# k times v as one product a head in two column groups: an RWKV-5 block with a feed-forward, on one core

## The chip, the cores and the metric

The kernel runs on one core of one Trainium2 chip. The metric is device time in microseconds (us) of one execution. The program has 24 units of work (four batches by six chunks of 128 tokens). Engines are named as the profile names them: PE is TensorE's matmuls, PEld its weight loads, DVE is VectorE, ACT ScalarE, POOL GpSimd, SP SyncE.

## The reference

```python
# attention: r, k, v of shape (4, 8, 768, 48); w, u of shape (8, 48)
state = np.zeros((B, H, D, D))
for t in range(S):
    cur = np.einsum('bhd,bhe->bhde', u[None] * kt, vt)
    y[:, :, t] = np.einsum('bhd,bhde->bhe', rt, state + cur)
    state = w[None, :, :, None] * state + np.einsum('bhd,bhe->bhde', kt, vt)
# then, on x of shape (3072, 384): h = x @ w_in (384 x 1024), SoLU, layer norm, ln @ w_out (1024 x 384)
```

The kernel works chunk by chunk. Within a chunk of 128 tokens the attention is a masked score matrix times v. Between chunks it carries a state of 48 by 48 a head, to which each chunk adds k (decayed) times v.

## The kernel before

Heads are padded from 48 to 64 columns in k and r, so that two heads fill the 128 partitions. The state of a pair of heads is a tile of 128 partitions by 2 x 48 columns, with each head's block on the diagonal. The rest of it must be zero, because y multiplies the whole tile. The product of k and v was taken for a pair of heads at once. Half of its result is one head's k with the other's v, and the weight tile `wt`, zero off the diagonal, removes it.

```python
def make_wt():                                   # called once, in the second step
    nc.gpsimd.memset(wt, 0.0)
    for q in range(2):
        rows = slice(q * P, q * P + D)
        nc.gpsimd.tensor_copy(out=wt[rows, :, q, :],
                              in_=pw[rows, 0, 7].unsqueeze(2).to_broadcast([D, HP, D]))
# ... in finish(i), after y_ps:
if c < C - 1:
    kv_ps = psM.tile([128, HP, 2, D], F32, tag="m", name="kv_ps")
    for a in range(HP):                          # four pairs of heads
        nc.tensor.matmul(kv_ps[:, a], pair(X["kp"], a), vt[:, 2 * a : 2 * a + 2, 0:D],
                         start=True, stop=True)
    if c > 0:
        nc.vector.tensor_add(St, kv_ps, St)
        nc.gpsimd.tensor_mul(St, St, wt)
    else:
        nc.vector.tensor_mul(St, kv_ps, wt)
# ... the order of one step of the loop, on TensorE:
# tr_ps, tk_ps (transposes of r and k), t_ps (of solu), h_ps, at (scores), o_ps, y_ps, kv_ps
```

## Time and profile before

| | before |
|---|---|
| median of 5 runs | 427.5 us (427.41 to 427.6) |
| span in the profile, mean granted clock | 425.5 us, 0.984 |
| TensorE busy | 396.0 us, 93% |
| kv_ps on the chain that ended last | 1.06 us a unit, 13 times |

The page has each engine's busy time, and the chain of work that ended last, followed back from the end. Two rows of such views carry the argument: a row of the busy table (a stretch of time, then busy us of each engine) says which engine is full, and a row of the chain (start, us, what) says what a piece of work costs where it counts. The prediction below shows these lines.

### The profile page before, as it was taken

To read this page: it belongs to the slowest core of one execution; us is meant where nothing else is said; L and a number is where in the kernel's file an instruction comes from. 1 tells how busy PE (TensorE), PEld (TensorE's weight loads), DVE (VectorE), ACT (ScalarE), POOL (GpSimd) and SP (SyncE) were. 2 spreads that over 40 slices of the span, in tenths; PEclk is the share of its full clock that TensorE was granted. 3 is DMA by queue.
4 is the path that set the end of the run, shared out by engine and by line. 5 is a ranking of instruction groups with operands and counts; after the bars stand their busy time and mean duration, and the time that the engine had idled before them with its cause. 6 is when DMAs were issued, how large, how long until landed. Compare 5 with 4: busy or idle time off the path is not lost.

```text
span 425.5 us, 7222 instructions
## 1 busy us (share of the span) xinstructions
PE 396.0 (93%) x2873; PEld 250.3 (59%) x2873; DVE 157.5 (37%) x302; ACT 181.6 (43%) x424; POOL 146.7 (34%) x220
## 2 busy tenths in 40 slices
PE   2699698879999999999999999999999999999994
PEld 2576255545756656656656656666666655556662
DVE  5988566635332352242242242242242321122110
ACT  1965666662524524525525525525525522233210
POOL 4886556556244144144135135135131100111000
PEclk9999899997999999999999999999999999999998
DMA  8999794000123034034034034034000000000101
GB/s 167 284 182 254 136 166 76 20 2 0 28 47 76 24 52 76 20 56 76 19 56 76 14 62 76 6 70 75 2 18 20 19 2 20 19 20 18 37 18 46
DMA packets 81592, 25.92 MB, mean 61 GB/s; under 512 B 76557, under 2 KB 79758, under 8 KB 81550
## 3 DMA queue, kind: packets, MB, share of 16 engines
q1 hardware_dynamic: 81406, 25.18, 29.6%
q8 instruction: 24, 0.39, 0.4%
q10 hardware_dynamic: 144, 0.20, 0.2%
q14 instruction: 18, 0.15, 0.1%
HBM read 20.65 MB, written 4.72 MB: 60 GB/s over the span
## 4 chain that ended last, share of the span: by engine, by line
PE 78%; DVE 9%; ACT 8%; POOL 2%; issue 2%; DMA 1%; ACTq 0%; POOLq 0%
PE o_ps L816 30%; PE h_ps L774 24%; PE y_ps L744 7%; PE t_ps L805 5%; PE at L716 4%; ACT AT L691 3%; PE kv_ps L760 3%; DVE ma L524 2%; PE tk_ps L705 2%; DVE ma L526 2%; PE tr_ps L697 2%; DVE AT L719 1%; DVE mag L520 1%; DVE solu L786 1%; ACT e L788 1%
## 5 line engine op out<-in xcount | busy, mean ns | idle before, releaser
L774 PE MATMUL h_ps<-w_in_sb,xT 128*128 128x512 f32 x288 | 129.6, 599 | 4.0 <-DVE solu L786 4.0
L816 PE MATMUL o_ps<-w_out_sb,lnT 128*128 128x384 f32 x384 | 129.5, 491 | 0.0
L816 PEld LDWEIGHTS o_ps<-w_out_sb,lnT 128*128 128x128 f32 x384 | 71.2, 190 | 47.5 <-issue 1.0
L774 PEld LDWEIGHTS h_ps<-w_in_sb,xT 128*128 128x128 f32 x288 | 53.4, 193 | 63.1 <-issue 62.2
L719 DVE COPY_PREDICATED AT<-later,at 128x512 f32<-128x512 uint32 x48 | 32.1, 721 | 92.0 <-ACT e L777 89.0
L777 ACT ACTIVATE e<-h_ps 128x1024 f32<-128x1024 f32 x24 | 24.6, 1023 | 89.9 <-PE h_ps L774 89.9
L691 ACT ACTIVATE AT<-ident,own 128x128 f32<-128x128 f32 x192 | 58.4, 386 | 0.8 <-DVE own L685 0.8
L788 ACT ACTIVATE e<-solu 128x1024 f32<-128x1024 f32 x24 | 25.4, 1057 | 71.0 <-DVE solu L786 71.0
L790 POOL TENSOR_TENSOR st<-st 128x1 f32<-128x1 f32 x24 | 4.7, 194 | 139.6 <-DVE solu L786 139.6
L716 PEld LDWEIGHTS at<-rT,kT 48*128 48x128 f32 x384 | 25.7, 198 | 18.7 <-issue 15.5
L763 DVE TENSOR_TENSOR state<-kv_ps,state 128x384 f32<-128x384 f32 x16 | 8.9, 557 | 69.8 <-PE kv_ps L760 69.8
L674 POOL TENSOR_TENSOR kp<-kpad,kdec 128x512 f32<-128x512 f32 x24 | 31.7, 1323 | 5.1 <-ACT kdec L591 4.9
L764 POOL TENSOR_TENSOR state<-state,wt 128x384 f32<-128x384 f32 x16 | 16.1, 1006 | 47.5 <-DVE state L763 47.5
L716 PE MATMUL at<-rT,kT 48*128 48x128 f32 x384 | 30.7, 298 | 1.6 <-DVE AT L719 1.4
L786 DVE SCALAR_TENSOR_TENSOR solu<-h_ps,st,e 128x1024 f32<-128x1024 f32 x24 | 30.8, 1284 | 1.1
L807 DVE COPY lnT<-t_ps 128x512 f32<-128x512 f32 x24 | 16.4, 683 | 36.5 <-PE t_ps L805 36.5
L744 PE MATMUL y_ps<-AT,vt 128*32 128x128 f32 x768 | 27.6, 279 | 0.0
L819 ACT ACTIVATE o<-o_ps,st 128x384 f32<-128x384 f32 x24 | 13.6, 569 | 29.1 <-PE o_ps L816 14.0
L805 PE MATMUL t_ps<-ident,solu 128*128 128x128 f32 x192 | 25.9, 279 | 0.0
L706 ACT COPY kT<-tk_ps 128x512 f32<-128x512 f32 x24 | 14.0, 584 | 25.2 <-PE tk_ps L705 25.2
L805 PEld LDWEIGHTS t_ps<-ident,solu 128*128 128x128 f32 x192 | 22.6, 144 | 2.7 <-issue 2.0
L681 POOL TENSOR_TENSOR rku<-rku,rpad 128x384 f32<-128x384 f32 x23 | 23.3, 1015 | 1.8
(80 smaller groups left out, 378.8 us busy)
## 6 DMA issues: line engine op xcount, KB each, us to landing
kpad<-in_k_dram SPq DMA_DIRECT2D x24, 192.0 KB, 4.2
rpad<-in_r_dram SPq DMA_DIRECT2D x24, 192.0 KB, 4.0
vt<-in_v_dram SPq DMA_DIRECT2D x24, 192.0 KB, 4.1
out_dram<-o SPq DMA_DIRECT2D x24, 192.0 KB, 2.1
raw<-in_moe_w_in_dram SPq DMA_DIRECT2D x6, 512.0 KB, 5.5
raw<-in_moe_w_out_dram SPq DMA_DIRECT2D x8, 384.0 KB, 4.3
u_bc<-in_u_dram ACTq DMA_DIRECT2D x1, 192.0 KB, 3.8
wq<-in_w_dram SPq DMA_DIRECT2D x1, 1.5 KB
```

What stands on the lines that cost most here:

```text
L674: nc.gpsimd.tensor_mul(X["kp"].rearrange("p h d -> p (h d)"), kpads[i % NLD].rearrange("p h d -> p (h d)"), kdec.rearrange("p a d -> p (a ...
L681: engine.tensor_mul(rku, rku, rpads[i % NLD][:, :, 0:D])
L691: nc.scalar.activation(out=AT[:, h, :], in_=ident, func=ACT.Copy, scale=X["own"][:, h])
L716: nc.tensor.matmul(pss[q][:, a, :], X["kT"][rows, a, :], X["rT"][rows, a, :], start=True, stop=True)
L719: nc.vector.copy_predicated(A4[:, :, q, :], later.to_broadcast([128, HP, T]), pss[q])
L744: nc.tensor.matmul(y_ps[32 * g : 32 * g + 32, j, :], lhsT, rhs, start=(g not in opened), stop=stop, skip_group_check=True)
L774: nc.tensor.matmul(h_ps[:, ts(n, NX)], X["xT"][:, j, :], w_in_sb[:, j, ts(n, NX)], start=(j == 0), stop=(j == KD - 1))
L777: nc.scalar.activation(out=e, in_=h_ps, func=ACT.Exp, accum_out=sums[:, i : i + 1])
L786: nc.vector.scalar_tensor_tensor(out=solu, in0=X["h"], scalar=rs, in1=X["e"], op0=ALU.mult, op1=ALU.mult, accum_out=tot)
L788: nc.scalar.activation(out=X["e"], in_=solu, func=ACT.Square, accum_out=ss)
L805: nc.tensor.transpose(t_ps[:, f, :], X["solu"][:, ts(4 * g + f, 128)], ident)
L816: nc.tensor.matmul(o_ps, X["lnT"][:, f, :], w_out_sb[:, f, :], start=(f == 0), stop=(f == KF - 1))
```

## The change

One product a head: 64 columns of k (48 and 16 of padding) by 48 columns of v. The two heads of a pair go to the two halves of the partitions, which are two column groups of the array (a column group is a block of its columns that takes weights and products of its own; how the array is divided is called its tiling mode). Below, "drain" is the time in which earlier products finish before a change of mode, and an "exposed" weight load is one that no product hides. No block across heads is computed, so the weight tile isn't needed, but the states must now be zeroed once, and each half of the state is updated by itself.

```diff
-    wt = const.tile([128, HP, 2, D], F32, name="wt")
-    def make_wt(): ...                                        # cut
+    for St in states:
+        nc.gpsimd.memset(St, 0.0)
@@ finish
-            kv_ps = psM.tile([128, HP, 2, D], F32, tag="m", name="kv_ps")
+            kv_ps = psM.tile([128, HP, D], F32, tag="m", name="kv_ps")
             for a in range(HP):
-                nc.tensor.matmul(kv_ps[:, a], pair(X["kp"], a), vt[:, 2 * a : 2 * a + 2, 0:D],
-                                 start=True, stop=True)
-            if c > 0:
-                nc.vector.tensor_add(St, kv_ps, St)
-                nc.gpsimd.tensor_mul(St, St, wt)
-            else:
-                nc.vector.tensor_mul(St, kv_ps, wt)
+                for q in range(2):
+                    nc.tensor.matmul(kv_ps[ts(q, P), a], X["kp"][:, 2 * a + q, :],
+                                     vt[:, 2 * a + q, 0:D], start=True, stop=True)
+            for q in range(2):
+                wT = pw[ts(q, P), 0, 7].unsqueeze(2).to_broadcast([P, HP, D])
+                S = St[ts(q, P), :, q]
+                if c > 0:
+                    nc.vector.tensor_add(S, kv_ps[ts(q, P)], S)
+                    nc.gpsimd.tensor_mul(S, S, wT)
+                else:
+                    nc.vector.tensor_mul(S, kv_ps[ts(q, P)], wT)
```

More of the change, by code (lines that the diff above doesn't have):

```diff
@@ L602, in direct_path @@
     states = [const.tile([128, HP, 2, D], F32, name=f"state{b}") for b in range(B)]
-    wt = const.tile([128, HP, 2, D], F32, name="wt")
-    def make_wt():
-        nc.gpsimd.memset(wt, 0.0)
-        for q in range(2):
-            rows = slice(q * P, q * P + D)
-            nc.gpsimd.tensor_copy(out=wt[rows, :, q, :],
-                                  in_=pw[rows, 0, 7].unsqueeze(2).to_broadcast([D, HP, D]))
+    for St in states:
+        nc.gpsimd.memset(St, 0.0)
     N = len(units)
@@ L857, in direct_path @@
             weigh(i + 3, nc.gpsimd)
-        if i == -1:
-            make_wt()
         if i == 10:
```

## The prediction

> **What bounds the kernel now.** I read the page first: its first two parts and the chain that ended last. Then I read the busy table by stretch, the chain in order of time, and last the timeline around one product of k and v. On the page (columns: engine, busy us, share of the span, instructions) the matmul engine stands alone, and most of the chain is its work:
>
> ```profile
> PE 396.0 (93%) x2873; PEld 250.3 (59%) x2873; DVE 157.5 (37%) x302; ACT 181.6 (43%) x424; POOL 146.7 (34%) x220
> PE 78%; DVE 9%; ACT 8%; POOL 2%; issue 2%; DMA 1%; ACTq 0%; POOLq 0%
> ```
>
> The busy table by stretch (columns: stretch, its length, busy us of each engine, granted clock, DMA share, GB/s) says where that holds. From 98 us on TensorE is never idle, and VectorE, ScalarE and GpSimd are busy for a third of the time or little more:
>
> ```profile
> 98.00:114.00 16.00, 16.00 (x89) 10.22 (x91) 8.70 (x12) 6.02 (x15) 9.58 (x11) 0.89 0.00 0
> 114.00:323.00 209.00, 209.00 (x1623) 132.70 (x1618) 65.52 (x121) 87.32 (x209) 70.36 (x104) 1.00 0.25 47
> 323.00:425.00 102.00, 96.41 (x546) 57.47 (x536) 18.32 (x36) 28.37 (x55) 6.01 (x20) 0.99 0.06 23
> ```
>
> Before 98 us the chain is a mix of VectorE, ScalarE and GpSimd work, with no piece of the k-times-v product (kv_ps) on it. After that it is TensorE alone, one period per unit of 16.08 us (columns: start, us on the chain, what):
>
> ```profile
> 179.25 1.06 PE kv_ps L760 x8
> 180.31 0.44 PE tr_ps L697 x4
> 180.75 0.44 PE tk_ps L705 x4
> 181.19 0.87 PE t_ps L805 x8
> 182.06 5.15 PE h_ps L774 x12
> 187.21 1.09 PE at L716 x16
> 188.30 5.36 PE o_ps L816 x16
> 193.66 1.67 PE y_ps L744 x56
> ```
>
> There are 20 units with a kv product (five chunks of four batches). The chain in order of time has it 13 times, at 114.95, 131.02 and so on to 307.86 us. So what the change is worth is 13 times what it takes off the 1.06 us, plus whatever it does to the mixed start.
>
> The timeline around one of them (start, us, engine, line, what; the bracket is idle time before it) shows why eight small matmuls take 1.06 us:
>
> ```profile
> 194.16 0.90 PEld L744 LDWEIGHTS y_ps<-AT,vt 128*32 128x32 f32 x32
> 195.25 0.97 PEld L760 LDWEIGHTS kv_ps<-vt,kp 128*128 128x128 f32 x8 [0.20 <-issue]
> 196.12 0.47 PEld L697 LDWEIGHTS tr_ps<-ident,rpad 128*128 128x128 f32 x4
> ```
>
> Each fp32 product appears as two weight loads and two matmuls, so 4 products are 8 pairs. Eight loads take 0.97 us and the last one lasts 0.192 (the median of the rows for kv_ps), so one starts every (0.97 - 0.192) / 7 = 0.111 us. The streamed operand is 96 columns. The 384-column products of o_ps take 5.36 / 16 = 0.335 us on the chain, or 0.87 ns a column, so 96 columns need about 0.084 us. **The weight load of 128 columns sets the pace, not the stream.** In the y_ps row, 32 loads into four column groups take 0.90 us: eight rounds of four, one round every (0.90 - 0.11) / 7 = 0.113 us. Four groups therefore run at once. The score products, with two row groups, do the same: 16 loads in the 0.97 us of 8.
>
> **What the Trainium skill says.** (1) "TensorE: Matmul & The Clock Gate", LDWEIGHTS: the load lasts about P/1.2 ns, where P is the number of columns, whatever the contraction. That is 107 ns for 128 columns; the trace agrees with its pitch of 111. It is 53 ns for 64. The durations agree with the slope: 0.110 us for 32 columns against 0.192 for 128 is 0.85 ns a column. (2) "TensorEngine Tiling (Array Packing)", Key Properties: tiles load and multiply independently, and changing the tiling mode drains the engine. The rounds of four in y_ps agree with the first; the 0.20 us of idle before the kv loads, just after the 32-column mode, with the second. (3) "VectorE: DVE Perf Modes", on the errata: an fp32 two-tensor op takes (N + 151) / 0.96 ns. For N = 384 that is 557 ns, and the trace has 557 for the state sum. (4) "PSUM — Partial Sum Buffer", bank collisions: different column tiles may write one bank at the same time on disjoint partitions. That is what the new kv_ps asks for, and what y_ps does already with 32 columns.
>
> **The change part by part.**
>
> TensorE. It removes 4 products a unit, 128 columns of k by 96 of v, of which half (one head's k by the other's v) was thrown away. It adds 8 products, 64 columns of k by 48 of v, alternating between two column groups: 16 pairs in place of 8.
> - Stream: 48 columns at 0.87 ns are 0.042 us. Load: half of 107 ns plus the 4 ns by which the pitch exceeds it, 0.058 us. The load still sets the pace within a column group.
> - Each group has 8 pairs, 8 x 0.058 = 0.46 us. I take the two groups to run side by side, as the four of y_ps do.
> - Around this: the drain after y_ps, which is there today too. From the end of the last y stream to the first kv load I read about 0.09 us (the last y matmul starts at 195.05 and streams 0.107). Then comes a **new** mode change, from 64-column tiles to the full array of the transposes: about 0.04 for the last stream, 0.09 of drain, and an exposed weight load of the first transpose, about 0.06.
> - Sum from the end of the y stream to the first transpose's stream: 0.09 + 0.46 + 0.04 + 0.09 + 0.06 = 0.74 us. Today the same stretch is 195.16 to 196.22, which is 1.06. **Gain 0.32 us a unit; 13 of them on the path make 4.1 us.**
>
> VectorE. One op of 557 ns on 128 x 384 becomes two on 64 x 192; columns count, partitions do not. By the formula each is (192 + 151) / 0.96 = 357 ns. Consecutive ops overlap by about 0.09 (the 558 ns sum starts at 180.35 and the next op at 180.82), so the pair takes 0.27 + 0.36 = 0.63 against 0.56: 0.07 more, on an engine idle for two thirds of the steady stretch. The sum can start 0.4 earlier, as its matmuls end earlier.
>
> GpSimd. 1.006 us for 384 columns and 1.295 for 512 give 2.26 ns a column and 0.14 fixed. Two of 192 are about 1.14 us: 0.13 more, and nothing on the path waits for them before the next chunk of that batch, four units later. The four zeroings of the states (four of about 0.42, the measured zeroing of the weight tile of the same size) fall before the first decay of k at 8.84 us, where GpSimd waits 4.9 us. The weight tile's three ops at 21.8 to 23.1 us go, but the next op waited for a load that landed at 23.32, so their time turns into waiting. Both worth about nothing.
>
> Start. Up to 98 us VectorE, ScalarE and GpSimd set the pace, so an earlier kv gains nothing. Once, at 82.5 us, the k transpose on TensorE waits. The page names GpSimd, but the transpose also waits on VectorE, whose state sum ends at 82.45, the kv buffer being reused. There the pair of ops costs up to 0.07 on the path. I charge 0.1 us.
>
> Total: 427.5 - 4.1 + 0.1 = **423.5 us**, or 0.9% less.
>
> **The rivals.**
>
> (a) The two 64-column groups do not overlap, or 16 pairs are limited by issue. Then kv takes 16 x 0.058 = 0.93 us plus the new drain, 1.21 in all: 0.15 worse, times 13, about 429.5 us. For it: more instructions, and no 64-column tile in this trace. Against it: y_ps sustains a pair every 0.113 / 4 = 0.028 us, and the new product needs one every 0.029.
>
> (b) A 64-column load costs no more than a 32-column one, since its halves go in at once; then the stream of 42 ns sets the pace: 8 x 0.044 = 0.35, another 0.11 a unit, 422.1 us. Nothing in the trace favours it beyond the four-way overlap in y_ps.
>
> (c) A new wait: the second half of the solu transposes (t_ps) takes the PSUM buffer of kv_ps and so waits for VectorE. Its load waits on VectorE's semaphore at 197.43 today, and the state sum ends at 196.98, a margin of 0.44. After the change TensorE arrives about 0.32 earlier, at 197.11. The last kv matmul should be visible to VectorE at about 195.97, so the pair ends at about 196.6: margin 0.5. This bites only if a half takes over 0.6 us. If it did, most of the gain would be lost and the time would be 426 to 427.
>
> (d) The gain is real and far larger because the path also shortens at the start: against it, no kv piece before 98 us on the chain. A gain of 2% needs 8.6 us, or 0.65 on each of 13 units; the products would have to take 0.4 us including two drains.
>
> **Range and chances.** Rival (b) and a little luck at the start give 421.7; a dearer mode change (0.1 more on 13 units) and some loss at the start give 425.5. I widen slightly to 421.5 to 426.0. Two per cent faster is out of reach of the sum (0.03). Two per cent slower would need rival (a) much worse than worked out (0.02). The rest, 0.95, is within 2%.
>
> **What would show it.** In the profile after: the chain's period of 16.08 us should be about 15.76, with kv_ps at about 0.5 and a larger share for the transpose after it. Weight loads of 64 columns should last about 0.137 us (0.110 + 32 x 0.85 ns), and 16 of them take about 0.55 us on the timeline, in pairs side by side. An idle time before the loads of tr_ps should appear, about as large as the one before kv_ps. The state ops should show 0.36 us on VectorE, and no idle time at t_ps. The start should reach the TensorE-bound stretch at 98 us as now. The prediction is wrong if the 16 loads take about 1 us (a), if t_ps gets a wait on the state (c), or if the stretch before 98 us moves by more than a microsecond.

## The result, and the profile after

The changed kernel took 423.53 us, the median of 5 runs (423.33 to 423.92), against 427.5 beside it. The ratio is 0.9904, with a 95% interval of 0.9891 to 0.9918. A ratio here is the mean time of one kernel's fast runs over that of the other's fast runs of the same rounds, so it is not quite the ratio of the medians. The difference is clear of the noise, and smaller than 2%.

The engines' line and the chain's shares, from the page of the changed kernel:

```profile
PE 388.5 (92%) x3033; PEld 242.2 (57%) x3033; DVE 162.8 (39%) x322; ACT 181.3 (43%) x424; POOL 147.5 (35%) x237
PE 77%; DVE 10%; ACT 5%; issue 3%; POOL 2%; DMA 1%; ACTq 0%; POOLq 0%
```

TensorE has 160 more matmuls (eight a unit) and 7.5 us less busy time; VectorE has 5.3 us more. The busy table shows the same bound as before: TensorE never idles from 98 us to 323 us.

```profile
98.00:114.00 16.00, 16.00 (x82) 10.08 (x84) 8.78 (x12) 5.74 (x14) 9.51 (x11) 0.89 0.00 1
114.00:323.00 209.00, 209.00 (x1783) 131.30 (x1772) 70.12 (x137) 89.83 (x214) 70.85 (x117) 1.00 0.25 48
```

The chain in order of time, one period of it (start, us, what):

```profile
178.30 0.60 PE kv_ps L754 x16
178.90 0.59 PE tr_ps L690 x4
179.49 0.44 PE tk_ps L698 x4
179.92 0.87 PE t_ps L802 x8
...
192.40 1.67 PE y_ps L737 x56
194.06 0.60 PE kv_ps L754 x16
```

The kv piece went from 1.06 to 0.60 us, and the transposes behind it went from 0.44 to 0.59: that 0.15 is the new change of tiling mode. Everything else in the period is as it was. The timeline of the weight loads shows both (start, us, engine, line, what, and idle time before it):

```profile
177.13 0.89 PEld L737 LDWEIGHTS y_ps<-AT,vt 128*32 128x32 f32 x32
178.23 0.55 PEld L754 LDWEIGHTS kv_ps<-vt,kp 128*64 128x64 f32 x16 [0.20 <-issue]
178.83 0.42 PEld L690 LDWEIGHTS tr_ps<-ident,rpad 128*128 128x128 f32 x4
```

Sixteen loads take 0.55 us and each lasts 0.138, so eight rounds of two start every (0.55 - 0.138) / 7 = 0.059 us: the two groups run side by side.

Over 11 periods, from the ninth kv product to the last, the period is 16.076 us before and 15.767 after. That is 0.309 less, and 13 times it is 4.0 us. The times differ by 3.97. But the start is **not** as before. The timeline of the first microseconds has this on GpSimd and VectorE of the changed kernel:

```profile
3.71 1.49 POOL L604 MEMSET state<- 128x384 f32 x4
```

```profile
4.44 0.94 DVE L580 COPY tab<-pw 128x4 f32<-128x4 f32 x1
4.51 0.86 DVE L577 TENSOR_TENSOR pw<-pw 128x4 f32<-128x4 f32 x1
4.59 0.79 DVE L578 RECIPROCAL pw<-pw 128x4 f32<-128x4 f32 x1
```

and on VectorE of the kernel before:

```profile
4.32 0.17 DVE L580 COPY tab<-pw 128x4 f32<-128x4 f32 x1
```

A copy of four columns took 0.94 us in place of 0.17, with the two ops behind it, and it ended just after GpSimd's zeroings did. So the first decay of k started at 9.72 in place of 8.84 us. The product of the column means, which comes just before the TensorE-bound part, started at 97.64 in place of 96.67. Then most of this was given back by the clock. That product runs after 4 us of idle TensorE. In the profile before, the granted clock was 0.50 during it; in the profile after it was 0.88. Below are the chain's line for it and the busy table for just that stretch (the third number from the end is the granted clock), first before, then after:

```profile
96.67 1.65 PE mean_ps L659 x2
96.67:98.32 1.65, 1.65 (x3) 0.94 (x4) 0.00 (x0) 0.00 (x0) 0.00 (x0) 0.50 0.00 0
```

```profile
97.64 0.96 PE mean_ps L652 x2
97.64:98.60 0.96, 0.96 (x3) 0.65 (x4) 0.00 (x0) 0.00 (x0) 0.00 (x0) 0.88 0.00 0
```

The first transposes of the TensorE-bound part follow at 98.32 before and 98.60 after. The start therefore lost 0.97 us, of which 0.28 was left. The last scaling of an output (o) starts at 419.58 before and 415.85 after: 3.73 us, which is 4.0 less 0.28.

### The profile page after: what moved, and what is told of

Same layout as the page of the kernel before. It is cut to its first block, busy times and chain, and to the rows that moved or that the text cites. A ratio compares the mean times of both kernels' runs of the same rounds, so it can differ in the third digit from the quotient of the medians.

```text
span 421.8 us, 7597 instructions
## 1 busy us (share of the span) xinstructions
PE 388.5 (92%) x3033; PEld 242.2 (57%) x3033; DVE 162.8 (39%) x322; ACT 181.3 (43%) x424; POOL 147.5 (35%) x237
## 4 chain that ended last, share of the span: by engine, by line
PE 77%; DVE 10%; ACT 5%; issue 3%; POOL 2%; DMA 1%; ACTq 0%; POOLq 0%
PE o_ps L813 30%; PE h_ps L771 24%; PE y_ps L737 7%; PE t_ps L802 5%; PE at L709 4%; DVE ma L524 2%; ACT AT L684 2%; PE tr_ps L690 2%; PE tk_ps L698 2%; DVE ma L526 2%; PE kv_ps L754 2%; DVE mag L520 2%; DVE AT L712 1%; DVE solu L783 1%; ACT e L785 1%
## 5 line engine op out<-in xcount | busy, mean ns | idle before, releaser
L760 DVE TENSOR_TENSOR state<-kv_ps,state 64x192 f32<-64x192 f32 x32 | 11.4, 355 | 63.6 <-PE kv_ps L754 63.0
L761 POOL TENSOR_TENSOR state<-state,pw 64x192 f32<-64x192 f32 x32 | 16.1, 504 | 39.8 <-DVE state L760 38.6
L673 POOL TENSOR_TENSOR rku<-kpad,u_bc 128x384 f32<-128x384 f32 x23 | 23.5, 1021 | 0.0
```

What stands on the lines that cost most here:

```text
L673: engine.tensor_mul(rku, kpads[i % NLD][:, :, 0:D], u_bc)
```

## The experiments

All eleven runs gave correct results. They ran in three groups, each group on one chip beside the kernel before. Each is the changed kernel with the edit shown; run 5 has none. The theory: the gain is made on TensorE alone, by weight loads half as wide in two groups that run at once, less a new mode change, and the zeroing costs time at the start. The rivals are named with each run.

### 1. The old products, the new halves

```diff
+            kv_ps = psM.tile([128, HP, 2, D], F32, tag="m", name="kv_ps")
             for a in range(HP):
+                nc.tensor.matmul(kv_ps[:, a], pair(X["kp"], a), vt[:, 2 * a : 2 * a + 2, 0:D], start=True, stop=True)
# the halves read kv_ps[ts(q, P), :, q]
```

> The four products of 128 by 96 columns are put back; the halves of the state and the zeroing of the states at the start stay. Theory (the gain is the matmul engine's alone, and the zeroing costs up to 0.9 us at the start because it blocks a VectorE copy): 427.5 to 428.4 us, kv_ps back to 1.06 us a unit on the chain. Rival (the gain comes from the state update by halves or from the removed weight tile): clearly under 427 us.

Measured: 427.56 us, beside 427.27 for the kernel before; ratio 1.0012 (0.9999 to 1.0025). The period is 16.076 us again, kv_ps 1.06 us on the chain. So nothing of the gain comes from the halves, from the lost weight tile or from GpSimd.

### 2. The zeroing moved to where the weight tile was made

```diff
-    for St in states:
-        nc.gpsimd.memset(St, 0.0)
@@ the loop
+        if i == -1:
+            for St in states:
+                nc.gpsimd.memset(St, 0.0)
```

> The changed kernel, with the four zeroings of the states moved from about 3.7 us to where the weight tile was made before (about 22 us). Theory (VectorE's small table copy at 4.4 us took 0.94 instead of 0.17 us because GpSimd's zeroings held a port that both need): the copy is back to about 0.17 us, the k transposes start 0.8 to 0.9 us earlier, and the time falls by 0.3 to 0.9 us to 422.6 to 423.2. Rival (the late start is chance, or is absorbed before 98 us): 423.5 us.

Measured: 424.2 us, ratio 0.9929 (0.9916 to 0.9941). The expectation missed. The copy did take 0.17 us again and k's decay started at 8.89 us, but the gain was lost at 22 us. The timeline there:

```profile
21.82 1.49 POOL L855 MEMSET state<- 128x384 f32 x4
...
21.98 1.60 DVE L520 TENSOR_SCALAR mag<-mag 128x512 f32<-128x512 f32 x1
```

The scaling `mag` takes 0.53 us in the kernel before and 0.40 in the changed one; here it took 1.60 and ended 0.28 us after the last zeroing. The same stall came back at another place. It isn't peculiar to zeroing: in the kernel before, the next `mag`, at 23.61 us, took 1.52 us behind GpSimd's decay of k (23.32 to 24.85 us).

The Trainium skill tells of the mechanism, which I had not looked up when I predicted. In "SBUF — State Buffer", Who interferes with whom, it says that VectorE's copies and scalings can use a port pair that GpSimd shares, and that whoever issues first holds the pair and the other blocks fully. Both stalls fit that: a copy and a scaling, each begun behind a zeroing. The page adds that ScalarE never waits. That is tried in run 8.

### 3. One column group after the other

```diff
-            for a in range(HP):
-                for q in range(2):
+            for q in range(2):
+                for a in range(HP):
```

> The changed kernel, with the eight products in another order: all four of the first column group, then all four of the second. Theory A (each column group takes its instructions as soon as it is free, whatever the order of the program): kv_ps stays at 0.60 us and the time at 423.5. Theory B (matmuls start in program order, so overlap needs alternation): the second group waits for the first, 0.46 us more on 13 units, 429.5 us; half of that if only some of the pairs can pass.

Measured: 426.75 us, ratio 0.9995 (0.9982 to 1.0008). The chain has

```profile
195.37 0.87 PE kv_ps L754 x16
```

for each unit, 0.27 more than with alternation, and the period is 16.033. Neither theory holds alone. The trace doesn't name the column group of a matmul, but its starts fall into two series of eight, each 0.058 us apart after a first step of 0.094. The second series starts 0.275 us after the first, when five of the first eight have started; from there on both run side by side. I take the two series to be the two groups. So the order of the program need not be the order in which groups start, but the look ahead is limited, and without alternation nearly the whole gain of the change is lost. The first half of this disagrees with "TensorE: Matmul & The Clock Gate", Part 3, which says that matmuls start strictly in program order. What limits the look ahead is open.

### 4. A wider stream

```diff
-            kv_ps = psM.tile([128, HP, D], F32, tag="m", name="kv_ps")
+            kv_ps = psM.tile([128, HP, P], F32, tag="m", name="kv_ps")
@@
-                                     vt[:, 2 * a + q, 0:D], start=True, stop=True)
+                                     vt[:, 2 * a + q, 0:P], start=True, stop=True)
```

> The changed kernel, with 64 columns of v streamed in place of 48 (the 16 more are zeros and are not read). Theory (the weight load of 64 columns sets the pace at 0.058 us a pair, and a stream of 64 columns needs 0.055): no change, 423.5 us, pairs still 0.058 apart. Rival (the stream is part of the pace): 16 columns at 0.87 ns are 0.014 us more on each of 8 rounds and 13 units, 1.4 us, 424.9 us.

Measured: 424.05 us, ratio 0.9924 (0.9911 to 0.9938). The period is 15.780 us, 0.013 longer, where a stream-paced product would have added 0.11. So 64 columns of v are nearly as cheap as 48, and the load sets the pace. The half microsecond above 423.53 is not the edit's, as the next run shows: here the product of the means started at 97.84 and ran at a granted clock of 0.50,

```profile
97.84 1.65 PE mean_ps L652 x2
```

and the TensorE-bound part began at 99.49 us, 0.89 later than in the profile of the changed kernel. The same work met another granted clock.

### 5. The changed kernel again

> The changed kernel itself, unedited, as the reference for the three runs beside it on this chip: 423.5 us, give or take 0.5. If it were 424 or more, the first four runs' excess over 423.5 would be the chip's and not their edits'.

Measured: 424.1 us, ratio 0.9923 (0.9909 to 0.9937). Its runs fall into two groups, 423.5 and 423.9 to 424.2. That is the reference for the next three, and it means that a difference of 0.5 us between two of these kernels proves nothing; the periods and the milestones in the traces do.

### 6. Four column groups

```diff
             for a in range(HP):
                 for q in range(2):
-                    nc.tensor.matmul(kv_ps[ts(q, P), a], X["kp"][:, 2 * a + q, :],
-                                     vt[:, 2 * a + q, 0:D], start=True, stop=True)
+                    for n in range(2):
+                        nc.tensor.matmul(kv_ps[ts(2 * q + n, 32), a], X["kp"][:, 2 * a + q, ts(n, 32)],
+                                         vt[:, 2 * a + q, 0:D], start=True, stop=True)
```

> The changed kernel, with each product cut once more, into two of 32 columns of k: 16 products in four column groups, the tiling that y_ps before it already has. Theory (a change of tiling mode costs a drain and an exposed weight load; the stream of 0.044 us then sets the pace in each group): no idle time before kv_ps, 8 rounds of 0.044, the period down by 0.2 to 0.26 us, 13 times: 420.2 to 421.0 us. Rival (TensorE cannot start pairs faster than the one per 0.028 us of y_ps): 32 pairs take 0.87 us, about 0.1 us a unit worse than now, 424.9 us.

Measured: 421.62 us, ratio 0.9871 (0.9854 to 0.9889), against 0.9923 for run 5. The weight loads:

```profile
192.97 0.89 PEld L737 LDWEIGHTS y_ps<-AT,vt 128*32 128x32 f32 x32
193.84 0.49 PEld L755 LDWEIGHTS kv_ps<-vt,kp 128*32 128x32 f32 x32
194.40 0.42 PEld L690 LDWEIGHTS tr_ps<-ident,rpad 128*128 128x128 f32 x4
```

There is no idle time before kv_ps any more: y_ps and kv_ps share one mode. On the chain kv_ps is 0.34 us for 32 pairs, and a period is 15.50 us (178.63 to 194.13), 0.26 less. The theory held at both ends. A mode change avoided is worth its drain, and the pairs of four groups start every 0.0106 us on average, so the 0.028 of y_ps was no limit of issue. Its median is 2.5 us below run 5's; between the two profiled executions, 423.5 and 421.41, it is 2.1. That is less than 13 times 0.26 (3.4). The trace accounts for 1.1 of the difference: this run's product of the means had a granted clock of 0.50, so that its TensorE-bound part began at 99.21 us, run 5's at 98.38, and one of its periods took 15.75 us, because there o_ps waited for VectorE, which did a check of the inputs.

### 7. The scores next to y

```diff
-        if 0 <= i + 1 < N:
-            scores(i + 1)
         column_sums(fs)
@@
             ffn_out(l)
+        if 0 <= i + 1 < N:
+            scores(i + 1)
         if 0 <= i < N:
             finish(i)
```

> The changed kernel, with the score products moved from before o_ps to between o_ps and y_ps: the same work, one change of tiling mode fewer a unit (h_ps and o_ps are then neighbours in the full array). Theory (a change to the full array or to row groups costs 0.09 of drain and 0.11 of exposed weight load): 0.2 us on some 16 units, 420.3 us. Rival (the later scores make VectorE's masking late, and something waits for it; or the drain comes back elsewhere): 423.5 us or more.

Measured: 417.67 us, ratio 0.9774 (0.976 to 0.9787). The chain:

```profile
182.02 5.16 PE o_ps L813 x16
187.19 1.09 PE at L709 x16
188.28 1.67 PE y_ps L737 x56
```

o_ps is 5.16 us behind h_ps, where it was 5.36 behind the scores: the 0.2 of one mode change. The period is 15.57 us. The rest of the gain, which I had not expected, is at the start. There VectorE set the pace, and it did the two masks of the scores, 1.25 us on the chain, before the solu product that everything waits for. With the scores later the solu comes first. From the first solu to the fifth it is 43.1 us, where run 5 takes 46.1, and the product of the means starts at 93.38 in place of 97.46.

### 8. The states zeroed by ScalarE

```diff
-    for St in states:
-        nc.gpsimd.memset(St, 0.0)
@@ after the identity is made
+    for St in states:
+        for a in range(HP):
+            nc.scalar.activation(out=St[:, a].rearrange("p q d -> p (q d)"),
+                                 in_=ident[:, 0 : 2 * D], func=ACT.Copy, scale=0.0)
```

> The changed kernel, with the states zeroed by ScalarE in its idle time before 8 us, in place of GpSimd. Theory (GpSimd's zeroings block VectorE's copies and scalings of SBUF data at whatever time they run: 0.77 us at 4.4 us, and 1.07 us at 22 us in the run that moved them there; ScalarE blocks nobody): the table copy takes 0.17 us, the scaling at 22 us 0.4 to 0.5, the fourth-unit k transpose starts 0.7 to 0.9 us earlier than in the changed kernel (82.7 to 82.9 in place of 83.6) and the time is 422.6 to 423.2, unless the clock's state near 98 us takes it away. Rival (zeroing is no cause): no milestone moves, 423.5 us.

Measured: 422.18 us, ratio 0.9882 (0.9864 to 0.99), against 0.9923 for run 5. VectorE's timeline has both ops at their usual length:

```profile
4.56 0.17 DVE L585 COPY tab<-pw 128x4 f32<-128x4 f32 x1
```

```profile
22.18 0.41 DVE L520 TENSOR_SCALAR mag<-mag 128x512 f32<-128x512 f32 x1
```

So the stall is GpSimd's zeroing, at whatever time it runs. The k transpose that waits at 82.6 us before, and at 83.39 in run 5, starts at 82.86. The last output scaling is 0.54 us earlier than in run 5. The medians differ by more, some 1.9 us, and the spans of the two profiles by 1.35. Of this the trace has the other 0.8 after that last scaling: in the final handshake of the engines ScalarE answers about 1.0 us earlier. I don't know why; ScalarE's program is 16 instructions longer, and both runs with this edit show it. What the zeroing itself cost is thus about half a microsecond here.

### 9. All three

The edits of runs 6, 7 and 8 together.

> The three edits that paid, together: products in four groups of 32 columns (2.5 us less beside the changed kernel), scores between o_ps and y_ps (6.4 less), states zeroed by ScalarE (0.5 less in the trace, 1.9 in the times). If they add: 424.1 - 2.5 - 6.4 - 0.5 to 1.9, 413.3 to 414.7 us, period 15.3 us. Rival (they share a cause, above all at the start, where scores and zeroing both shorten VectorE's path): 415 to 417 us.

Measured: 413.9 us (412.4 to 413.96), ratio 0.9669 (0.9649 to 0.9688). They add, and the period is 15.31 us (189.64 to 204.95 on the chain; one took 15.80, as one of run 6 took 15.75). This version beats both kernels: 3.3% below the kernel before.

### 10. A slower state sum

```diff
-                    nc.vector.tensor_add(S, kv_ps[ts(q, P)], S)
+                    for a in range(HP):
+                        nc.vector.tensor_add(S[:, a], kv_ps[ts(q, P), a], S[:, a])
```

> The changed kernel, with each half of the state sum cut into four ops of 64 by 48 (first chunks excepted). Theory (the update is hidden, because the second group of solu transposes, which takes the buffer of kv_ps, comes 0.3 to 0.4 us after the pair of sums ends): eight ops of some 0.21 to 0.23 us end about 1.1 us later than the pair, so a wait on the state of 0.6 to 0.9 us appears at t_ps in every unit of the steady part, 8 to 12 us in all: 432 to 436 us. Rival (nothing on the matmul engine depends on that sum in time): 423.5 to 424.5 us.

Measured: 424.94 us, ratio 0.9942 (0.9924 to 0.9959). The size missed, since the small ops of one half overlap: they last 0.20 us but start every 0.115 to 0.13, so the eight take 1.16 us where the pair takes 0.74. That is 0.42 more and just uses up the margin: in the steady part t_ps grows from 0.87 to 0.90 us. In the trace its second group's load, which waits on VectorE, starts at 197.37, right after the last sum ends at 197.32. So the wait of rival (c) is real and was 0.3 to 0.4 us away. At the start the k transpose waits too: the chain of this run has it straight behind the sums.

```profile
84.19 0.60 DVE state L761 x4
84.78 0.14 issue
84.92 0.63 PE tk_ps L698 x4
```

It starts at 84.92, 1.35 us later than in the changed kernel: 0.42 from these sums, and 0.92 because they themselves start later. The same wait is on the chain a unit earlier, at 72.10 us, and h_ps behind it had a mean granted clock of 0.78 in this run, against 1.00 in the changed kernel, so part of the 0.92 is the clock's. Before and after, the profile named GpSimd as the releaser of that transpose; this shows that it is VectorE's state sum.

### 11. The products twice

```diff
+            for a in range(HP):
+                for q in range(2):
+                    nc.tensor.matmul(...)        # the same eight products once more
```

> The changed kernel, with the eight products issued twice over, the second writing the same values. Theory (16 pairs cost 8 x 0.058 us, drains and exposed loads come once): kv_ps grows from 0.60 to 1.06 us, 13 times: 6.0 us, 430.1 us. Rival (part of what the pairs cost is the drain and the first load, or the wait for the engine before): clearly less than 0.4 us a unit.

Measured: 430.67 us, ratio 1.0068 (1.0049 to 1.0086). The period is 16.233, 0.466 more, which is 8 x 0.0583 us. The products' own cost is what was predicted, and the rest of the 0.75 us between y_ps and the first transpose's stream is drains and exposed loads.

## Why the prediction was right, point by point

- **The bound.** Right: a kv piece of TensorE is on the chain 13 times and counts in full; run 1 shows that nothing else of the change gained.
- **The pace of a pair.** Right: 0.058 predicted, 0.0583 measured (run 11), set by the load (run 4; with loads of 32 columns, in run 6, it fell to 0.0425) with two groups at once. One reading was a little off: the 5.36 us of o_ps, from which the prediction took 0.87 ns a column, hold the 0.2 us of a mode change, and run 7's 5.16 make it 0.84. Nothing rested on the difference. Run 3 adds a condition that the prediction passed over: the program must alternate.
- **The new mode change.** Right: 0.15 predicted for drain and exposed load after kv_ps, and tr_ps grew by 0.15 on the chain. The trace before had that cost already: at 323.93 us, where tr_ps follows y_ps directly, it takes 0.59 and not 0.44.
- **The gain a unit.** 0.32 predicted, 0.309 measured.
- **VectorE's pair.** Mis-sized: 0.63 predicted, 0.74 measured. Each op took 0.356 as the formula gives (0.357), but the second half starts only after the first has ended, 0.38 later. The overlap of 0.09, read from ops on all partitions, did not carry over; it was hidden in the steady part.
- **GpSimd's pair.** 1.14 predicted, 1.00 measured (two of 0.502), and hidden.
- **The zeroing is free.** Wrong. The step put it into GpSimd's idle time and asked only what GpSimd delays by it in its own queue. It stalled VectorE's copy by 0.77 us (runs 2 and 8).
- **The start.** 0.1 charged. The milestone before the TensorE-bound part came 0.97 us later: about 0.8 from the stall, as VectorE's first op on solu and the state sum at 82 us start 0.77 and 0.79 later, and about 0.2 from the pair of ops at the k transpose, which follows the start of the state sum by 0.88 in place of 0.70. The prediction had up to 0.07 for that pair. That the total came within 0.1 us of the middle of the forecast is in part luck: the clock at 97 us gave back 0.69 of it in the profiled run. Without it the kernel seems to take 424.1 us, still inside the range: run 5's times fall into these two groups, and run 4's trace has the lower clock there. Run 5's ratio, 0.9923, is a gain of 3.3 us in place of 4.0.
- **The rivals.** (a) and (b) did not happen. For 64 columns the load, not the stream, set the pace; run 6 reached the pace that (b) describes with narrower groups. (c) was near, and run 10 reached it. Of (d) nothing came with this change, but run 7 shows that the start can be shortened by 4 us with another order.

## What to carry to other kernels

For small fp32 products on a full TensorE, count weight loads, not multiplications: cut the stationary operand into column groups, alternate between them in the program, and keep neighbours in the same tiling mode, because each change cost 0.15 to 0.2 us here. An op put into an idle engine is free only if it blocks no other engine meanwhile: look at what VectorE does while GpSimd works. When VectorE or ScalarE paces a stretch, ask first in which order it does its work; one reorder gained more than the change studied.

## What the Trainium skill lacked or had wrong

- "TensorE: Matmul & The Clock Gate" says that matmuls start strictly in program order. Across column groups they seem not to: in run 3, if its two series of starts are the two groups, the second group's first matmul started when only five of the first group's eight, all earlier in the program, had started.
- The same page has a floor of about 25 ns from start to start, however small the matmul, and about 4 ns between tiles of a divided array. It has no sustained rate for the latter. In run 6 a round of four starts came 6 to 7 ns apart and each group had a start every 42.5 ns: 32 pairs in 0.34 us, 10.6 ns each.
- "TensorEngine Tiling (Array Packing)" says that a mode change drains the engine and gives no cost. Here it was 0.15 us before transposes and 0.2 before products in the full array.
- "SBUF — State Buffer" says that the port pair is held for the whole instruction. It doesn't say what GpSimd instructions in a row do. The zeroings started every 0.36 us and lasted 0.42, so that they overlapped, and the VectorE copy waited for both that were left (0.94 us), not for one.
